# A long-convolution generator on one core: phases and exponents as pairs of PSUM banks, with exponential and absolute value in one operation of 1024 columns

## The chip, the core and the metric

The kernel runs on one core of a Trainium2 chip. A core has a matrix engine (TensorE, PE in the profile; its weight loads are PEld), a vector engine (VectorE, DVE), an engine for functions of one operand (ScalarE, ACT), a general one (GpSimd, POOL) and one that issues transfers (SyncE, SP). Each works through its own queue in order, and waits for others through semaphores. TensorE writes its results to PSUM, which has eight banks of 512 float32 columns in each of 128 partitions; the other operands lie in SBUF. The metric is the time of one execution on the device, in microseconds.

## The reference, cut to what matters

All is float32, for 2048 tokens of 448 channels. The first half is a state-space convolution, of which the kernel K is what the change touches:

```python
dt = jnp.exp(log_dt)
A = -jnp.exp(log_A_real) + 1j * A_imag              # 448 x 256
C = (C_real + 1j * C_imag) * dt[:, None]
P = jnp.exp((A * dt[:, None])[:, :, None] * pos)    # pos = 0 .. 2047
K = 2.0 * jnp.einsum("dn,dnl->dl", C, P).real       # 448 x 2048
y = irfft(rfft(u_t, 4096) * rfft(K, 4096))[:, :, :2048]
```

Around it stand a modulation (`silu(c) @ w_mod`, cut into six vectors), a layer norm ahead of the convolution, a gated residual, a second layer norm, and a two-layer perceptron over the tokens (2048 to 1792 to 2048, with gelu), gated into the residual.

## The kernel before, in words

**Generator.** A position is written as 64 j + i, so that P is a product of a part E (over j, 64 values) and a part G (over i, 32 values), each a magnitude times a cosine or sine. The 448 channels are 28 groups of 16, and a group's 256 states are two halves of 128 partitions; so there are 56 steps s, of 16 channels x 128 states each (16 channels x 32 values = 512 columns). A step needs two exponents (for E and G) and two phases (for E and G), each a full PSUM bank of 128 x 512.

- `st_exponents` (L612) has TensorE compute the exponents of E and of G from a small table and the parameters (`lex`), by `halves` (L606): partitions 0 to 63 of the operands give E's, 64 to 127 G's, two matmuls that can run side by side. `st_exp` (L617) has ScalarE take two exponentials, L621, into one SBUF tile `mag` of 2 x 512 columns.
- `st_phase` (L623) gives the phases in turns, reduced to within half a turn by adding and subtracting a large constant in PSUM: eight matmuls, four for each bank.
- `st_mag2` (L634) has GpSimd form `m2`, the magnitudes for the second half of E, in two operations (L637, L639).
- `st_step` (L642) has ScalarE take two absolute values (L651 of E's phase into `ab`, L652 of G's into a `gs` buffer) and four sines: E's sine (L653, in place in PSUM), G's sine (L654), G's cosine (L655) and E's cosine (L656, into G's phase bank), the cosines being sines of a quarter turn less the absolute value. GpSimd forms G by two products (L658, L659), VectorE E by four: L660 and L661 with the sine, then whatever `between()` has queued for VectorE, then L663 and L664 with the cosine.
- `st_kgen` (L676) multiplies G and E on TensorE into 32 x 64 blocks of K, which ScalarE copies out (L699); `st_s1` (L710) starts K's transform.

The PSUM pool `pph` has two buffers each of a bank `xe` and a bank `xg`, used in turn by exponents and phases; so phases of step s+2 reuse the banks of step s. `ab` has one buffer, `gs` three, `m2` three (and five more, `m2l`, from s = 32), `mag` eight.

**Order.** Exponentials and sines need different tables on ScalarE, so the steps are taken in seven windows of eight (`BATCH`): `window(s)` at s = 0, 8, ..., 48 takes eight exponentials, with TensorE one exponent ahead, and then eight steps follow. The order on TensorE, ScalarE, VectorE and GpSimd is that in which the program writes its instructions (a manual schedule); SP's order is left to the scheduler from s = 8 to the end of the generator. In iteration s the phases of s+1 are written ahead of step s; from s = 33 on, `st_kgen(s - 1)` is between them. Other work is written into the same queues: until s = 32 the parameters of the next channels (`chain`, in pieces on VectorE, with `split`, L379, whose two-part results `hl` are stored by SP's queue at L388 and come back as `lph` and `lex`), the modulation, the transform of the input (`u_rows`, `u_cols`), and from s = 32 the inverse transform of the first 224 channels (`piece`: `pc_s2` and `pc_inv` on TensorE, the products L786 on VectorE).

**After the generator**, from about 367 us of the span, come the inverse transform of the other channels, the second layer norm and the two large products of the perceptron (L1191 to L1193 and L1333 to L1335), each weight split into two parts by ScalarE (L206) and VectorE (L215).

Of the kernel before, what the change touches and what calls it, by code (L numbers as in the profile page):

```python
# [11 lines left out]
F32 = mybir.dt.float32  # L12
F32R = mybir.dt.float32r
# [9 lines left out]
P = 128  # L23
# [4 lines left out]
GD = 16  # L28
# [192 lines left out]
def tile_adaln_s4d_mixer(ctx, tc, i, out):  # L221
# [20 lines left out]
    with ExitStack() as es:  # L242
# [126 lines left out]
        def chain(q):  # L369
# [7 lines left out]
            )  # L377

            def split(src, places):  # L379
                hl = qp.tile([P, 2, N], F32R, tag="hl", name="hl", bufs=3)[:, :, 0:f]  # L380
                eng = G if aside else V
                eng.tensor_copy(hl[:, 0], src)
                yield
                eng.tensor_tensor(hl[:, 1], src, hl[:, 0].bitcast(F32), ALU.subtract)
                for k, v in places:
                    for m in range(P // n):
                        to = pars[q][v, k, 0:n, :, m * f : (m + 1) * f]
                        nc.sync.dma_start(to, hl[n * m : n * m + n].bitcast(F32))  # L388
                yield
# [216 lines left out]
        def halves(out, lhs, rhs, start, stop):  # L606

            for k in range(2):
                r = slice(64 * k, 64 * k + 64)
                T.matmul(out[k], lhs[r], rhs[r], start=start, stop=stop)  # L610

        def st_exponents(s):  # L612
            g, h = divmod(s, 2)
            phs[s] = [pph.tile([P, 512], F32, tag=nm, name=nm) for nm in ("xe", "xg")]
            halves(phs[s], lex[g % 4][:, h * P : (h + 1) * P], tab[:, 2], True, True)

        def st_exp(s):  # L617
            mags[s] = mp.tile([P, 2, 512], F32, tag="mag", name="mag")
            pm = phs.pop(s)
            for k in range(2):  # L620
                S.activation(mags[s][:, k], pm[k], AF.Exp)  # L621

        def st_phase(s):  # L623

            g, h = divmod(s, 2)
            lhs = lph[g % 3][:, h * P : (h + 1) * P]
            pm = [pph.tile([P, 512], F32, tag=nm, name=nm) for nm in ("xe", "xg")]
            halves(pm, lhs, tab[:, 1], True, False)
            halves(pm, mg[:, 0], ones, False, False)
            halves(pm, mg[:, 1], ones, False, False)  # L630
            halves(pm, lhs, tab[:, 0], False, True)
            phs[s] = pm

        def st_mag2(s):  # L634
            me = v32(mags[s][:, 0])
            w = wp.tile([P, GD], F32, tag="w", name="w")
            G.tensor_tensor(w[:, :, None], me[:, :, 31:32], me[:, :, 1:2], ALU.mult)  # L637
            m2 = m2p[s >= 32 and s % BATCH > 2].tile([P, GD, 32], F32, tag="m2", name="m2")
            G.tensor_tensor(m2, me, w[:, :, None].to_broadcast([P, GD, 32]), ALU.mult)  # L639
            m2s[s] = m2  # L640

        def st_step(s, between):  # L642
            me, mg_, m2 = v32(mags[s][:, 0]), v32(mags[s][:, 1]), m2s.pop(s)
            E = gp_.tile([P, 2, GD, NJ], F32, tag="E", name="E")
            Gt = gp_.tile([P, 2, GD, NI], F32, tag="G", name="G")


            xe, xg = phs.pop(s)
            ab, sg, cg_ = (wp.tile([P, 512], F32, tag=nm, name=nm, bufs=b) for nm, b in (("ab", 1), ("gs", 3), ("gs", 3)))

            S.activation(ab, xe, AF.Abs)  # L651
            S.activation(cg_, xg, AF.Abs)  # L652
            S.activation(xe, xe, AF.Sin, scale=TWO_PI)  # L653
            S.activation(sg, xg, AF.Sin, scale=-TWO_PI)  # L654
            S.activation(cg_, cg_, AF.Sin, scale=-TWO_PI, bias=math.pi / 2)  # L655
            S.activation(xg, ab, AF.Sin, scale=-TWO_PI, bias=math.pi / 2)  # L656
            se, ce = v32(xe), v32(xg)
            G.tensor_tensor(Gt[:, 1], mg_, v32(sg), ALU.mult)  # L658
            G.tensor_tensor(Gt[:, 0], mg_, v32(cg_), ALU.mult)  # L659
            V.tensor_tensor(E[:, 1, :, 32:64], m2, se, ALU.mult)  # L660
            V.scalar_tensor_tensor(E[:, 1, :, 31::-1], me[:, :, 31::-1], -1.0, se, ALU.mult, ALU.mult)  # L661
            between()
            V.tensor_tensor(E[:, 0, :, 31::-1], me[:, :, 31::-1], ce, ALU.mult)  # L663
            V.tensor_tensor(E[:, 0, :, 32:64], m2, ce, ALU.mult)  # L664
            eg[s] = (E, Gt)
            mags.pop(s)
# [297 lines left out]
        def window(s):  # L964
# [13 lines left out]
            for e in range(BATCH):  # L978
# [37 lines left out]
                    piece(pieces[0] < NP)  # L1016
                if s == 0 and e in (4, 5):
                    st_mag2(e - 4)
                elif s and (e < 2 or s >= 32):
                    st_mag2(s + e)  # L1020
                if s == 8 and e == 0:
                    u_norm(e + 2)
# [13 lines left out]
        for s in range(tail):  # L1036
            if s == 32:
                early.close()
                fp = es.enter_context(tc.tile_pool(name="fp", bufs=2))
                m2p.append(right("m2l", BATCH - 3))  # L1040
                yks[1] = fp.tile([P, 32, DC], F32, name="yk1", bufs=1)
                for n in range(3):
                    pc_load(n)
# [44 lines left out]
            free = s > 7 and not st_s1(s % BATCH == BATCH - 1)  # L1088
            if s + 2 < 32 and (s + 2) % BATCH > 1:
                st_mag2(s + 2)  # L1090

            if 3 < s < 8:
                modulation(s // 2 - 1, s % 2)
# [273 lines left out]
```

## Time and profile before

| | |
|---|---|
| time, median of 3 runs | 719.54 us (715.1 to 722.51) |
| the profiled execution, its own time | 720.75 us |
| its span, first to last instruction | 719.0 us |
| mean granted TensorE clock | 0.962 |
| busy: PE, ACT, DVE, POOL | 648.0, 453.1, 431.4, 271.7 us |
| first and last L651 (absolute value of step 0, step 55) | 30.03 and 361.14 us |

A group's row names line, engine, operation, output <- input, shape and count, then busy time and mean duration (ns), and after the second bar the idle time of the engine just before and what ended most of it. A row of a timeline is: start in us from the span's beginning, duration in us, engine, line, operation, output <- input; in brackets, idle time before it and what ended it. The chain names the work that ended last, step by step back from the end. Durations of neighbours on one engine can overlap, so the distance from start to start says what an operation costs in a row of them.

### The profile page before, as it was taken

To read this page: it belongs to the slowest core of one execution; us is meant where nothing else is said; L and a number is where in the kernel's file an instruction comes from. 1 tells how busy PE (TensorE), PEld (TensorE's weight loads), DVE (VectorE), ACT (ScalarE), POOL (GpSimd) and SP (SyncE) were. 2 spreads that over 40 slices of the span, in tenths; PEclk is the share of its full clock that TensorE was granted. 3 is DMA by queue.
4 is the path that set the end of the run, shared out by engine and by line. 5 is a ranking of instruction groups with operands and counts; after the bars stand their busy time and mean duration, and the time that the engine had idled before them with its cause. 6 is when DMAs were issued, how large, how long until landed. Compare 5 with 4: busy or idle time off the path is not lost.

```text
span 719.0 us, 18067 instructions
## 1 busy us (share of the span) xinstructions
PE 648.0 (90%) x7090; PEld 479.3 (67%) x7090; DVE 431.4 (60%) x821; ACT 453.1 (63%) x849; POOL 271.7 (38%) x341
## 2 busy tenths in 40 slices
PE   0777999879979879898999979999999999999997
PEld 0443444435535556575679936778999999999996
DVE  7668768758577567584855448778622263334441
ACT  4877487887986989999947649787522242222220
POOL 5395657548656866867745600000000000000000
PEclk9998758998999989999999999999999999999999
DMA  8494545556867656555459999984585436555540
GB/s 196 154 200 130 194 141 178 204 162 197 250 194 237 186 119 178 147 156 156 137 156 282 296 255 251 248 218 115 171 231 150 145 110 175 168 159 154 154 142 26
DMA packets 99395, 128.00 MB, mean 178 GB/s; under 512 B 13546, under 2 KB 80622, under 8 KB 99310
## 3 DMA queue, kind: packets, MB, share of 16 engines
q1 hardware_dynamic: 97726, 122.78, 60.3%
q0 software_dynamic: 1008, 3.54, 2.2%
q8 instruction: 56, 0.92, 0.6%
q10 hardware_dynamic: 576, 0.52, 0.3%
q14 instruction: 29, 0.24, 0.1%
HBM read 91.46 MB, written 34.87 MB: 176 GB/s over the span
## 4 chain that ended last, share of the span: by engine, by line
PE 65%; ACT 12%; DMA 9%; DVE 6%; issue 3%; POOL 3%; SPq 1%; DVEq 0%; ACTq 0%; POOLq 0%
PE acc L1191 6%; PE o L1333 6%; PE o L1335 6%; PE o L1334 6%; PE acc L1193 6%; PE acc L1192 6%; PE xe L610 6%; PE kg L685 4%; DMA wm<-in_w_mod_dram 4%; PE vv L794 3%; PE kx L778 3%; PE vv L795 3%; PE pu L563 2%; PE xg L610 2%; PE pm L487 2%
## 5 line engine op out<-in xcount | busy, mean ns | idle before, releaser
L206 ACT CAST whi<-w 128x896 fp32r<-128x896 f32 x64 | 59.8, 937 | 135.5 <-PE o L1334 84.8
L658 POOL TENSOR_TENSOR G<-mag,gs 128x512 f32<-128x512 f32 x56 | 72.0, 1286 | 69.3 <-ACT gs L654 69.1
L215 DVE TENSOR_TENSOR wlo<-w,whi 128x896 fp32r<-128x896 f32 x64 | 68.0, 1086 | 43.2 <-ACT whi L206 37.0
L1191 PE MATMUL acc<-h3h,whi 128*128 128x448 f32 x224 | 82.8, 370 | 0.8 <-ACT h3h L1242 0.8
L1192 PE MATMUL acc<-h3l,whi 128*128 128x448 f32 x224 | 80.9, 361 | 0.7 <-DVE h3l L1249 0.5
L1193 PE MATMUL acc<-h3h,wlo 128*128 128x448 f32 x224 | 81.3, 363 | 0.0
L1333 PE MATMUL o<-uh,whi 128*128 128x448 f32 x224 | 81.3, 363 | 0.0
L1335 PE MATMUL o<-uh,wlo 128*128 128x448 f32 x224 | 81.2, 362 | 0.0
L1334 PE MATMUL o<-ul,whi 128*128 128x448 f32 x224 | 80.6, 360 | 0.0
L610 PE MATMUL xg<-tab,lph 64*128 64x512 f32 x112 | 66.7, 597 | 12.6 <-DVE E L664 7.7
L685 PEld LDWEIGHTS kg<-E,G 128*32 128x32 f32 x3584 | 56.7, 115 | 31.1 <-issue 16.4
L610 PE MATMUL xe<-tab,lph 64*128 64x512 f32 x112 | 65.7, 592 | 9.3 <-ACT gs L655 7.6
L659 POOL TENSOR_TENSOR G<-mag,gs 128x512 f32<-128x512 f32 x56 | 71.8, 1282 | 0.0
L685 PE MATMUL kg<-E,G 128*32 128x64 f32 x3584 | 66.5, 229 | 3.4 <-ACT ks L699 2.0
L660 DVE TENSOR_TENSOR E<-m,xe 128x512 f32<-128x512 f32 x56 | 38.4, 686 | 46.6 <-ACT xe L653 30.3
L639 POOL TENSOR_TENSOR m<-mag,w 128x512 f32<-128x512 f32 x56 | 58.7, 1049 | 4.4
L1337 DVE SCALAR_TENSOR_TENSOR y<-o,b,mod 128x448 f32<-128x448 f32 x16 | 11.0, 685 | 80.2 <-PE o L1335 80.2
L1191 PEld LDWEIGHTS acc<-h3h,whi 128*128 128x128 f32 x224 | 42.0, 188 | 12.8 <-ACT h L1247 5.6
L786 DVE TENSOR_TENSOR z<-kx,u 128x448 f32<-128x448 f32 x48 | 28.4, 620 | 32.5 <-PE kx L778 32.5
L610 PE MATMUL xe<-tab,lex 64*128 64x512 f32 x56 | 29.8, 544 | 19.7 <-DMA lex<-wm 18.1
L651 ACT ACTIVATE ab<-xe 128x512 f32<-128x512 f32 x56 | 33.9, 606 | 17.4 <-PE xg L610 9.9
L1192 PEld LDWEIGHTS acc<-h3l,whi 128*128 128x128 f32 x224 | 41.9, 187 | 4.1 <-DVE h3l L1249 0.8
(221 smaller groups left out, 1514.7 us busy)
## 6 DMA issues: line engine op xcount, KB each, us to landing
w<-in_B_w_dram SPq DMA_DIRECT2D x64, 224.0 KB
w<-in_B_w_dram SPq DMA_DIRECT2D x32, 448.0 KB
u<-us_d SPq DMA_DIRECT2D x48, 224.0 KB
yu_d<-yt SPq DMA_DIRECT2D x16, 448.0 KB
yi<-yu_d SPq DMA_DIRECT2D x32, 224.0 KB
us_d<-uo SPq DMA_DIRECT2D x16, 448.0 KB
v_d<-vt SPq DMA_DIRECT2D x32, 224.0 KB
vt<-v_d SPq DMA_DIRECT2D x16, 448.0 KB
```

What stands on the lines that cost most here:

```text
L206: self.nc.scalar.copy(hi, w)
L215: eng.tensor_tensor(lo, w, hi.bitcast(F32), ALU.subtract)
L610: T.matmul(out[k], lhs[r], rhs[r], start=start, stop=stop)
L658: G.tensor_tensor(Gt[:, 1], mg_, v32(sg), ALU.mult)
L659: G.tensor_tensor(Gt[:, 0], mg_, v32(cg_), ALU.mult)
L685: T.matmul(kgs[g][32 * q : 32 * q + 32, m], Gt[:, c, d], E[:, c, d], start=h == 0 and c == 0 and m == 0, stop=h == 1 and c == 1, skip_grou ...
L1191: nc.tensor.matmul(acc[f], hi[:, fs], h3h[:, r], start=r == 0, stop=False)
L1192: nc.tensor.matmul(acc[f], hi[:, fs], h3l[:, r], start=False, stop=False)
L1193: nc.tensor.matmul(acc[f], lo[:, fs], h3h[:, r], start=False, stop=r == 15)
L1333: nc.tensor.matmul(o, hi[:, ks], uh[kh][:, k], start=kh == 0 and k == 0, stop=False)
L1334: nc.tensor.matmul(o, hi[:, ks], ul[kh][:, k], start=False, stop=False)
L1335: nc.tensor.matmul(o, lo[:, ks], uh[kh][:, k], start=False, stop=kh == 1 and k == 6)
```

## The change

E's and G's banks become one tile `x` of two banks, from one pool tag with two buffers (the same four banks). One exponential and one absolute value of 2 x 512 columns take the place of two each. The four sines stay as they were, but the two cosines read their absolute value from the one tile `ab`, which is twice as large, with one buffer. To make room in SBUF, `hl` has two buffers in place of three and `m2l` four in place of five; for that, `m2` of the last step of each window from s = 32 is formed after the window's third step and not inside `window`.

```diff
-                hl = qp.tile([P, 2, N], F32R, tag="hl", name="hl", bufs=3)[:, :, 0:f]
+                hl = qp.tile([P, 2, N], F32R, tag="hl", name="hl", bufs=2)[:, :, 0:f]
...
-                T.matmul(out[k], lhs[r], rhs[r], start=start, stop=stop)
+                T.matmul(out[:, k], lhs[r], rhs[r], start=start, stop=stop)
 
         def st_exponents(s):
             g, h = divmod(s, 2)
-            phs[s] = [pph.tile([P, 512], F32, tag=nm, name=nm) for nm in ("xe", "xg")]
+            phs[s] = pph.tile([P, 2, 512], F32, tag="x", name="x")
...
         def st_exp(s):
             mags[s] = mp.tile([P, 2, 512], F32, tag="mag", name="mag")
-            pm = phs.pop(s)
-            for k in range(2):
-                S.activation(mags[s][:, k], pm[k], AF.Exp)
+            S.activation(mags[s], phs.pop(s), AF.Exp)
 
         def st_phase(s):
...
-            pm = [pph.tile([P, 512], F32, tag=nm, name=nm) for nm in ("xe", "xg")]
+            pm = pph.tile([P, 2, 512], F32, tag="x", name="x")
...
-            m2 = m2p[s >= 32 and s % BATCH > 2].tile([P, GD, 32], F32, tag="m2", name="m2")
+            m2 = m2p[s >= 32 and 2 < s % BATCH < 7].tile([P, GD, 32], F32, tag="m2", name="m2")
...
-            xe, xg = phs.pop(s)
-            ab, sg, cg_ = (wp.tile([P, 512], F32, tag=nm, name=nm, bufs=b) for nm, b in (("ab", 1), ("gs", 3), ("gs", 3)))
-
-            S.activation(ab, xe, AF.Abs)
-            S.activation(cg_, xg, AF.Abs)
+            x = phs.pop(s)
+            xe, xg = x[:, 0], x[:, 1]
+            ab = wp.tile([P, 2, 512], F32, tag="ab", name="ab", bufs=1)
+            sg, cg_ = (wp.tile([P, 512], F32, tag="gs", name="gs", bufs=3) for _ in range(2))
+
+            S.activation(ab, x, AF.Abs)
             S.activation(xe, xe, AF.Sin, scale=TWO_PI)
             S.activation(sg, xg, AF.Sin, scale=-TWO_PI)
-            S.activation(cg_, cg_, AF.Sin, scale=-TWO_PI, bias=math.pi / 2)
-            S.activation(xg, ab, AF.Sin, scale=-TWO_PI, bias=math.pi / 2)
+            S.activation(cg_, ab[:, 1], AF.Sin, scale=-TWO_PI, bias=math.pi / 2)
+            S.activation(xg, ab[:, 0], AF.Sin, scale=-TWO_PI, bias=math.pi / 2)
...
-                elif s and (e < 2 or s >= 32):
+                elif s and (e < 2 or s >= 32 and e < 7):
                     st_mag2(s + e)
...
-                m2p.append(right("m2l", BATCH - 3))
+                m2p.append(right("m2l", BATCH - 4))
...
+            if 32 <= s < NHALF and s % BATCH == 2:
+                st_mag2(s + 5)
```

In the changed kernel the line numbers from there on differ by one or two: the exponential is L619, the operations of a step on ScalarE are L651 (absolute value), L652 to L655 (sines), VectorE's products L659, L660, L662, L663, and GpSimd's G products L657, L658.

## Prediction

> **What bounds the kernel now.** I read the page's chain first, then its groups of instructions for the lines that the diff touches, then the timelines of ScalarE, VectorE and TensorE over one window of the generator, because the change lies in the generator alone (up to about 367 us of the span) and a share of the whole span says nothing about it.
>
> ```profile
> PE 65%; ACT 12%; DMA 9%; DVE 6%; issue 3%; POOL 3%; SPq 1%; DVEq 0%; ACTq 0%; POOLq 0%
> L660 DVE TENSOR_TENSOR E<-m,xe 128x512 f32<-128x512 f32 x56 | 38.4, 686 | 46.6 <-ACT xe L653 30.3
> L651 ACT ACTIVATE ab<-xe 128x512 f32<-128x512 f32 x56 | 33.9, 606 | 17.4 <-PE xg L610 9.9
> L206 ACT CAST whi<-w 128x896 fp32r<-128x896 f32 x64 | 59.8, 937 | 135.5 <-PE o L1334 84.8
> ```
>
> TensorE carries most of the chain, but most of that is the two big products after the generator, which the change only moves in time. In the generator the second row matters: VectorE, before its first product of a step, waits mostly (30.3 us of 46.6) for the FIRST sine of that step, L653, the third of ScalarE's six operations. The next fences show the last window of eight steps (s = 48 to 55). T(s) is the start of a step's L651.
>
> ```profile
> 334.76 0.60 ACT L651 ACTIVATE ab<-xe 128x512 f32<-128x512 f32 x1
> ...
> 338.66 0.60 ACT L656 ACTIVATE xg<-ab 128x512 f32<-128x512 f32 x1
> 339.30 0.60 ACT L651 ACTIVATE ab<-xe 128x512 f32<-128x512 f32 x1
> ...
> 341.77 0.61 ACT L656 ACTIVATE xg<-ab 128x512 f32<-128x512 f32 x1
> 342.30 0.55 ACT L800 COPY vt<-vv 128x448 f32<-128x448 f32 x1
> 342.72 0.62 ACT L651 ACTIVATE ab<-xe 128x512 f32<-128x512 f32 x1
> 343.20 0.63 ACT L652 ACTIVATE gs<-xg 128x512 f32<-128x512 f32 x1
> ...
> 344.19 0.64 ACT L654 ACTIVATE gs<-xg 128x512 f32<-128x512 f32 x1
> ...
> 345.19 0.65 ACT L656 ACTIVATE xg<-ab 128x512 f32<-128x512 f32 x1
> ...
> 349.79 0.63 ACT L651 ACTIVATE ab<-xe 128x512 f32<-128x512 f32 x1
> ...
> 357.23 0.63 ACT L651 ACTIVATE ab<-xe 128x512 f32<-128x512 f32 x1
> 361.14 0.61 ACT L651 ACTIVATE ab<-xe 128x512 f32<-128x512 f32 x1
> ```
>
> Two things are to be seen. First, operations of ScalarE that need not wait overlap: L651 starts at 342.72, lasts 0.62, and L652 starts at 343.20, 0.48 later. Second, an operation that waits for the one just before it loses that overlap: L656 at 341.77 is followed after 0.53 by a copy that does not need it, but L656 at 338.66 is followed after 0.64 by L651, which must wait until the single buffer of `ab` has been read. A step's last sine ends at 345.84, T + 3.12.
>
> ```profile
> 339.90 0.68 DVE L664 TENSOR_TENSOR E<-m,xg 128x512 f32<-128x512 f32 x1
> 344.42 0.69 DVE L660 TENSOR_TENSOR E<-m,xe 128x512 f32<-128x512 f32 x1 [0.71 <-ACT xe L653]
> 347.28 0.68 DVE L664 TENSOR_TENSOR E<-m,xg 128x512 f32<-128x512 f32 x1
> 354.34 0.68 DVE L664 TENSOR_TENSOR E<-m,xg 128x512 f32<-128x512 f32 x1
> ```
>
> ```profile
> 340.69 0.47 PE L610 MATMUL xg<-tab,lph 64*128 64x512 f32 x1 [0.97 <-DVE E L664]
> 348.16 0.50 PE L610 MATMUL xe<-tab,lph 64*128 64x512 f32 x1
> 348.76 0.58 PE L610 MATMUL xg<-tab,lph 64*128 64x512 f32 x1
> ```
>
> This is the loop that sets the pace of the steps, beside ScalarE's own work: there are two sets of phase banks, so the phases of step s+2 need the banks that the products of step s read last (L664). From the end of L664 to TensorE's next matmul is 0.11 us (339.90 + 0.68 = 340.58 to 340.69), the eight matmuls of a step take 1.18 (348.16 to 349.34), and ScalarE starts about 0.05 later: 1.34 us from the end of L664 to T(s+2) at the least.
>
> **The change part by part.** *One operation of 1024 columns for two of 512.* From 512 to 896 columns an operation goes from 606 to 937 ns, 0.86 ns a column, so 1024 columns are estimated at 1.05 us. Less the overlap of 0.13 that is 0.92 against two starts of 0.48: 0.04 saved per pair, 56 exponentials and 56 absolute values, 4.5 us if ScalarE set the pace everywhere. For the exponentials the gain lies between 0 and 56 x 0.04 = 2.2; TensorE shares the exponential windows, so I take 1.0.
>
> On ScalarE, the Trainium skill ("ScalarE: Activation LUTs", section "What ACT_TABLE_LOAD costs") gives 186 ns + 0.833 ns a column and an overlap of about 93 ns, so that a pair would save 93 ns: about 10 us over 112 pairs. The trace agrees with the page's duration (606 against 612), but its overlap here is 0.14, so less is left to save.
>
> *What the pair waits for.* The two banks are now one tile, `x`. The built program's order of ScalarE and VectorE, with each one's waits, shows what that does:
>
> ```
> ACT  L651 ab<-x     waits PE, and ACT L655 of the step before
> ACT  L652 x<-x      waits DVE (two steps back), and ACT L651, the operation just before
> ACT  L653 gs<-x     waits POOL, and ACT L652, the operation just before
> ACT  L654 gs<-ab    waits POOL
> ACT  L655 x<-ab     waits ACT L653
> DVE  L659 E<-m,x    waits ACT L655, the last sine of the step
> DVE  L660 E<-mag,x  no wait
> DVE  L662 E<-mag,x  no wait
> ```
>
> In the kernel before, the first product waited for L653 and the third for L656. Now all four stand behind the last sine, and two more of ScalarE's operations wait for their neighbour. A step on ScalarE becomes: absolute value 1.05 + 0.03, first sine 0.64, second 0.48, third 0.52, last 0.62 to its end, so the last sine ends at T + 3.34 where it was T + 3.12: 0.22 longer. VectorE's first product starts at T + 3.38 where it was T + 1.70 (344.42 - 342.72): 1.68 late, and with it the end of the products, since the work between them (the z products of L786, of the chain, of the evacuations) is queued behind the first two and starts as late. Where the third product already waited for the last sine (steps with nothing between), the delay is ScalarE's 0.22 and two products of about 0.6 (0.69 less some overlap), 1.4; in the first step of a window, where the table load stands before the sines and the last one moves from T + 4.50 (338.66 + 0.60 - 334.76) to T + 4.60, 1.30, and up to 1.68 where work lies between. Behind the waiting product stand, on VectorE's queue, the evacuations that TensorE needs; behind the phase matmuls on TensorE's queue stand `kgen` and the inverse transforms.
>
> *What of 1.68 reaches the next step but one.* T(s+2) moves by the delay less the slack, and the slack is T(s+2) less the end of L664 less 1.34. Last window: s = 48, 342.72 - 340.58 - 1.34 = 0.80, so 1.30 - 0.80 = 0.50; s = 50, 349.79 - 347.96 - 1.34 = 0.49, so 1.19; s = 52, 357.23 - 355.02 - 1.34 = 0.87, so 0.81. Sum 2.5, and 0.22 for the odd step at the end: 2.7. The window of s = 40 has the same rhythm, 26.36 against 361.14 - 334.76 = 26.38, so 2.7 again; that of s = 32 is 28.06 long for other waits, which can hide up to 1.7 of it; I take 1.7, between 1.0 and 2.7.
>
> ```profile
> 250.66 0.60 ACT L651 ACTIVATE ab<-xe 128x512 f32<-128x512 f32 x1
> ...
> 278.72 0.60 ACT L651 ACTIVATE ab<-xe 128x512 f32<-128x512 f32 x1
> 293.55 0.61 ACT L651 ACTIVATE ab<-xe 128x512 f32<-128x512 f32 x1
> ...
> 319.91 0.61 ACT L651 ACTIVATE ab<-xe 128x512 f32<-128x512 f32 x1
> ```
>
> The four windows before s = 32 have other bounds between, so only the tight loops count:
>
> ```profile
> 101.76 0.67 DVE L664 TENSOR_TENSOR E<-m,xg 128x512 f32<-128x512 f32 x1
> ...
> 124.54 0.68 DVE L664 TENSOR_TENSOR E<-m,xg 128x512 f32<-128x512 f32 x1
> ...
> 160.27 0.68 DVE L664 TENSOR_TENSOR E<-m,xg 128x512 f32<-128x512 f32 x1
> ...
> 226.80 0.68 DVE L664 TENSOR_TENSOR E<-m,xg 128x512 f32<-128x512 f32 x1
> ...
> 235.71 0.67 DVE L664 TENSOR_TENSOR E<-m,xg 128x512 f32<-128x512 f32 x1
> ```
>
> ```profile
> 103.56 0.60 ACT L651 ACTIVATE ab<-xe 128x512 f32<-128x512 f32 x1 [0.15 <-PE xe L610]
> ...
> 127.19 0.60 ACT L651 ACTIVATE ab<-xe 128x512 f32<-128x512 f32 x1
> ...
> 162.79 0.60 ACT L651 ACTIVATE ab<-xe 128x512 f32<-128x512 f32 x1 [1.31 <-PE xe L610]
> ...
> 230.35 0.60 ACT L651 ACTIVATE ab<-xe 128x512 f32<-128x512 f32 x1 [0.61 <-PE xe L610]
> ...
> 237.49 0.60 ACT L651 ACTIVATE ab<-xe 128x512 f32<-128x512 f32 x1 [0.75 <-PE xe L610]
> ```
>
> Window 24: from s = 27 the slack is 230.35 - 227.48 - 1.34 = 1.53, 0.15 comes through; from s = 29 it is 237.49 - 236.38 - 1.34 = -0.23 (TensorE there began one bank before the other was free, which a pair cannot), so 1.9; with 0.22, 2.3. Window 16: 162.79 - 160.95 - 1.34 = 0.50 after a first step, 1.1. Window 8: from s = 8, 103.56 - 102.43 - 1.34 = -0.21, 1.8, of which the queue on VectorE passes on about half by s = 13; there 127.19 - 125.22 - 1.34 = 0.63 lets 1.05 more through: 2.1. Window 0 ends in a wait for the modulation weights,
>
> ```profile
> 40.88 19.11 DMA wm<-in_w_mod_dram
> ```
>
> whose transfer starts once an early step has freed a table row on SP's queue: between 0 and 1.7, I take 0.4. After the last step the products end 1.4 later than 364.88 + 0.68 = 365.56, at 367.0, and `kgen`, which began at 365.89 behind GpSimd, begins about 1.2 later.
>
> ```profile
> 364.88 0.68 DVE L664 TENSOR_TENSOR E<-m,xg 128x512 f32<-128x512 f32 x1
> ...
> 365.89 0.93 PEld L685 LDWEIGHTS kg<-E,G 128*32 128x32 f32 x62 [0.41 <-POOL G L659]
> ```
>
> *The rest of the diff* pays for the larger `ab` with memory and I cost it at nothing. `hl` with two buffers makes a split wait for the store of two splits back instead of three; the chain's own arithmetic on VectorE lies between them and covers it; without that cover it is one store's landing on GpSimd per split. The late `st_mag2` of e = 7 goes to GpSimd's queue behind a step's G products, where GpSimd waits for the next sines anyway; without cover, one product per window. SP's order changes by a few places around s = 8 to 20, past loads that are needed a window later. Let each be worth 1 us either way.
>
> *Sum:* 0.4 + 2.1 + 1.1 + 2.3 + 1.7 + 2.7 + 2.7 + 1.2 - 1.0 = 13.2 us later at the end of the generator, and what follows is moved as a whole. The profiled execution took 720.75 (a span of 719.0 and 1.75 around it), 1.2 above the median of three, 719.54; so 734.0 by the one and 732.7 by the other. I say 733.5.
>
> **The rivals.** *Fewer instructions win (faster).* If the two banks were guarded apart, VectorE would start after the first sine as before, and only the saving would be left: 112 x 0.04 = 4.5, about 715. It decides if VectorE's first product starts under T + 2. Against it stands the order above, where the third product has no wait of its own. By the skill's overlap this rival would stand near 710. The Trainium skill ("PSUM — Partial Sum Buffer", "PSUM bank collisions raise a hardware error") asks for guards by bank and quadrant only, under which this rival would hold; the order shows guards wider than that. 0.05.
>
> *The delay is hidden (no change).* TensorE's own queue may be what each step waits for, and give the slack back: then only ScalarE's 0.22 in the 24 steps from s = 32 (5.3) and part of the end remain, at most 6, 722 to 726. For it: outside the tight loops the slacks are large, as 1.53 above. 0.17.
>
> *It spreads (slower still).* TensorE's queue is in order; if what stands behind the phases (inverse transforms, evacuations) gives no slack back, 1.7 comes through in three loops of each of seven windows: 36 us, 756; half of it, 18, and ScalarE's 5.3 give 744. 0.12.
>
> **How the numbers follow.** The forecast, 727 to 742, has 0.66. One per cent, about what a measurement of this kernel can tell from no change, is 712.3 to 726.7. Slower holds the forecast and the spreading: 0.78; the hidden delay is "same", 0.17; faster 0.05. The range takes in the upper part of the hidden case and the half-spread one: 725 to 746.
>
> **What would show it.** VectorE's group of the first product should name the last sine as its releaser and wait some 40 us or more for it, not 30.3. The 1024-column absolute value should last about 1.05 us, and each of the next two sines start after its predecessor's end. The windows of s = 40 and 48 should be 29 us long from first to last step, not 26.4. If they are 26.4 or less, the loop was not the bound and the forecast is wrong; if ScalarE sits idle before the 1024-column operations for TensorE by more than 1.5 us a step, the spreading is right.

## The result and the profile after

The changed kernel takes 752.0 us (median of 6 runs, 748.88 to 757.72); the kernel before takes 719.46 beside it (6 runs, 715.1 to 722.51). The ratio is 1.0458, with a 95% interval of 1.0417 to 1.05: it is slower, as forecast, but by 32.5 us and not by 13 to 14, and 752.0 lies over the range of 725 to 746. The profiled execution is the slowest of the six: 757.72 us, a span of 755.9, and a mean granted clock of 0.930 where it was 0.962 before. Where sizes matter I therefore go by stretches of the generator, and compare them over several kernels.

The first fence is from the page of the kernel after: the chain of work that ended last, and the groups that the change touches.

```profile
PE 60%; ACT 15%; DMA 9%; DVE 7%; issue 5%; POOL 3%; SPq 0%; ACTq 0%; DVEq 0%; POOLq 0%
L659 DVE TENSOR_TENSOR E<-m,x 128x512 f32<-128x512 f32 x56 | 38.5, 687 | 95.3 <-ACT x L655 49.1
L651 ACT ACTIVATE ab<-x 128x1024 f32<-128x1024 f32 x56 | 57.5, 1028 | 32.9 <-PE x L610 32.6
L619 ACT ACTIVATE mag<-x 128x1024 f32<-128x1024 f32 x56 | 55.6, 1026 | 23.8 <-PE x L610 20.0
```

VectorE's wait before its first product has doubled, 46.6 to 95.3 us. The page puts 49.1 of it down to L655, the step's last sine, and no longer to the first; the timeline shows the rest to be the same wait: the first product never starts before the last sine has ended, and in 53 of the 56 steps it starts 0.03 to 0.20 us after it, where in the kernel before it starts ahead of that end in 53 steps. The operations of 1024 columns last 1.03 us. The idle time before the absolute value, nearly all of it for TensorE, has grown from 17.4 to 32.9. The next three fences are timelines of the kernel after in the window of s = 40: ScalarE, VectorE and TensorE from the start of step 44 (T = 332.41) to that of step 45.

```profile
332.41 1.03 ACT L651 ACTIVATE ab<-x 128x1024 f32<-128x1024 f32 x1
333.48 0.58 ACT L652 ACTIVATE x<-x 128x512 f32<-128x512 f32 x1
334.15 0.60 ACT L653 ACTIVATE gs<-x 128x512 f32<-128x512 f32 x1
334.64 0.62 ACT L654 ACTIVATE gs<-ab 128x512 f32<-128x512 f32 x1
335.17 0.59 ACT L655 ACTIVATE x<-ab 128x512 f32<-128x512 f32 x1
337.06 0.37 ACT L698 COPY ks<-kg 128x256 f32<-128x256 f32 x1 [1.30 <-PE kg L684]
337.33 1.03 ACT L651 ACTIVATE ab<-x 128x1024 f32<-128x1024 f32 x1
```

```profile
333.95 0.68 DVE L663 TENSOR_TENSOR E<-m,x 128x512 f32<-128x512 f32 x1
335.85 0.69 DVE L659 TENSOR_TENSOR E<-m,x 128x512 f32<-128x512 f32 x1 [1.21 <-issue]
```

```profile
334.78 0.50 PE L610 MATMUL x<-tab,lph 64*128 64x512 f32 x2 [1.18 <-ACT gs L653]
335.09 0.60 PE L610 MATMUL x<-ones,mg 64*128 64x512 bf16 x3
...
335.89 1.10 PE L684 MATMUL kg<-E,G 128*32 128x64 f32 x64
```

Within a step all is as worked out: the absolute value 1.03, the first sine 0.04 after its end, the second 0.09 after the end of the first, the last sine done at 335.76 (T + 3.35, forecast T + 3.34), the first product at 335.85 (T + 3.44, forecast T + 3.38). What is new is the row before the last of ScalarE. It has nothing to do with the sines: L698 copies out a block of K, and stands in ScalarE's queue ahead of the next absolute value. Step 43's products end at 334.63, TensorE starts the phases of step 45 at 334.78, and these are there from about 336; but behind them on TensorE stands `kgen` of step 43, to 336.99, and ScalarE waits 1.30 us for it with the copy at the head of its queue. In the tables of ScalarE's waits (us in total, times, longest) this wait has nearly doubled; the first line is of the kernel before, the second of the kernel after:

```profile
ACT ks L699 <- PE kg L685: 9.3, 11, 2.5
ACT ks L698 <- PE kg L684: 17.7, 13, 2.4
```

From the end of the products to the next step but one are 337.33 - 334.63 = 2.70 us, not 1.34.

### The profile page after: what moved, and what is told of

It reads as the page before. It is cut to its first block, busy times and chain, and to the rows that moved or that the text cites. A ratio compares the mean times of both kernels' runs of the same rounds, so it can differ in the third digit from the quotient of the medians.

```text
span 755.9 us, 17908 instructions
## 1 busy us (share of the span) xinstructions
PE 653.7 (86%) x7090; PEld 480.1 (64%) x7090; DVE 426.7 (56%) x821; ACT 457.8 (61%) x737; POOL 272.5 (36%) x341
## 4 chain that ended last, share of the span: by engine, by line
PE 60%; ACT 15%; DMA 9%; DVE 7%; issue 5%; POOL 3%; SPq 0%; ACTq 0%; DVEq 0%; POOLq 0%
PE x L610 8%; PE acc L1192 6%; PE o L1334 6%; PE o L1336 6%; PE o L1335 6%; PE acc L1194 6%; PE acc L1193 6%; PE kg L684 5%; ACT ab L651 5%; DMA wm<-in_w_mod_dram 3%; PE pu L531 2%; ACT gs L653 2%; ACT x L652 2%; PE pm L487 2%; PE kx L777 2%
## 5 line engine op out<-in xcount | busy, mean ns | idle before, releaser
L610 PE MATMUL x<-tab,lph 64*128 64x512 f32 x224 | 73.5, 647 | 43.9 <-ACT gs L653 18.2
L657 POOL TENSOR_TENSOR G<-mag,gs 128x512 f32<-128x512 f32 x56 | 71.7, 1280 | 99.1 <-ACT gs L653 98.7
L659 DVE TENSOR_TENSOR E<-m,x 128x512 f32<-128x512 f32 x56 | 38.5, 687 | 95.3 <-ACT x L655 49.1
L684 PEld LDWEIGHTS kg<-E,G 128*32 128x32 f32 x3584 | 61.3, 123 | 31.9 <-issue 23.3
L651 ACT ACTIVATE ab<-x 128x1024 f32<-128x1024 f32 x56 | 57.5, 1028 | 32.9 <-PE x L610 32.6
L684 PE MATMUL kg<-E,G 128*32 128x64 f32 x3584 | 71.0, 239 | 1.6 <-DVE E L663 1.1
L658 POOL TENSOR_TENSOR G<-mag,gs 128x512 f32<-128x512 f32 x56 | 71.8, 1282 | 0.0
L610 PEld LDWEIGHTS x<-tab,lph 64*128 64x128 f32 x224 | 27.1, 227 | 70.0 <-ACT gs L653 24.1
L619 ACT ACTIVATE mag<-x 128x1024 f32<-128x1024 f32 x56 | 55.6, 1026 | 23.8 <-PE x L610 20.0
L610 PE MATMUL x<-tab,lex 64*128 64x512 f32 x112 | 32.3, 567 | 29.7 <-DMA lex<-wm 18.8
L785 DVE TENSOR_TENSOR z<-kx,u 128x448 f32<-128x448 f32 x48 | 28.4, 620 | 31.2 <-PE kx L777 31.2
```

What stands on the lines that cost most here:

```text
L610: T.matmul(out[:, k], lhs[r], rhs[r], start=start, stop=stop)
L651: S.activation(ab, x, AF.Abs)
L684: T.matmul(kgs[g][32 * q : 32 * q + 32, m], Gt[:, c, d], E[:, c, d], start=h == 0 and c == 0 and m == 0, stop=h == 1 and c == 1, skip_grou ...
```

## The experiments

Twelve more kernels ran. The table gives for each the ratio to the kernel before on the same chip, and, from its trace, the time from the first to the last L651 of some of the windows, and in the last column the gap from the last L651 of the window of s = 24 to the first of the next.

| kernel | us, ratio (95%) | s=8 | s=16 | s=24 | s=32 | s=40 | s=48 | gap |
|---|---|---|---|---|---|---|---|---|
| before | 719.46 | 32.4 | 30.1 | 34.4 | 28.1 | 26.4 | 26.4 | 13.2 |
| after | 752.0, 1.0458 (1.0417 to 1.05) | 39.1 | 31.1 | 37.0 | 32.1 | 31.9 | 32.6 | 18.0 |
| 1 before, cosine first | 744.07, 1.0352 (1.0272 to 1.0432) | 37.5 | 30.7 | 34.7 | 31.2 | 32.0 | 32.4 | 15.4 |
| 2 after, singles | 754.2, 1.0475 (1.0418 to 1.0531) | 37.6 | 31.8 | 34.9 | 33.3 | 32.9 | 32.7 | 19.0 |
| 3 before, memory | 720.62, 1.0004 (0.9977 to 1.0031) | 32.4 | 30.0 | 35.0 | 27.6 | 26.4 | 27.6 | 13.2 |
| 4 after, copy later | 744.68, 1.0335 (1.0285 to 1.0386) | 35.9 | 31.3 | 37.2 | 30.1 | 29.7 | 29.0 | 18.3 |
| 5 after, sine apart | 763.54, 1.0586 (1.0535 to 1.0638) | 40.1 | 35.7 | 38.8 | 31.0 | 32.0 | 31.0 | 18.4 |
| 5c after, room alone | 760.49, 1.0553 (1.0514 to 1.0593) | 39.2 | 31.4 | 36.1 | 32.1 | 31.9 | 32.6 | 19.1 |
| 6 after, both apart | 800.61, 1.1118 (1.1051 to 1.1185) | 44.6 | 41.1 | 41.0 | 35.0 | 36.3 | 36.3 | 14.3 |
| 7 before, both apart | 798.97, 1.1119 (1.1051 to 1.1186) | 42.2 | 41.2 | 41.1 | 35.0 | 35.2 | 36.1 | 14.4 |
| 8 after, other work first | 746.26, 1.0372 (1.0314 to 1.0431) | 31.4 | 29.7 | 36.2 | 33.6 | 32.4 | 32.6 | 18.0 |
| 9 after, 8 and 4 | 736.72, 1.0211 (1.0146 to 1.0277) | 31.4 | 30.1 | 36.4 | 29.3 | 29.3 | 29.2 | 18.0 |
| 10 before, copy later | 719.75, 0.9991 (0.9962 to 1.002) | 30.5 | 30.5 | 34.4 | 26.1 | 26.0 | 25.5 | 14.6 |
| 11 after, products early, 4 | 761.46, 1.0595 (1.0557 to 1.0633) | 37.0 | 34.9 | 36.7 | 32.8 | 33.2 | 33.2 | 18.0 |

The theory on trial (A): the two banks under one guard put all four products behind the last sine; that and what it pushes back in three in-order queues is the loss. The rivals: the long operation itself; the memory edits; the pair of banks, which can only be refilled as a whole.

**1. The products late, without any pair.** In the kernel before, VectorE takes the two products with the cosine first:

```diff
-            V.tensor_tensor(E[:, 1, :, 32:64], m2, se, ALU.mult)
-            V.scalar_tensor_tensor(E[:, 1, :, 31::-1], me[:, :, 31::-1], -1.0, se, ALU.mult, ALU.mult)
-            between()
             V.tensor_tensor(E[:, 0, :, 31::-1], me[:, :, 31::-1], ce, ALU.mult)
             V.tensor_tensor(E[:, 0, :, 32:64], m2, ce, ALU.mult)
+            between()
+            V.tensor_tensor(E[:, 1, :, 32:64], m2, se, ALU.mult)
+            V.scalar_tensor_tensor(E[:, 1, :, 31::-1], me[:, :, 31::-1], -1.0, se, ALU.mult, ALU.mult)
```

> The kernel before with nothing paired; VectorE's four products of a step stand in the other order, the two with the cosine first, so that all four stand behind the step's last sine. Theory A (the late products set the new time: in the changed kernel the first product starts at T + 3.4 and not T + 1.7): the first product starts at about T + 3.15 here, 1.45 late where the change makes it 1.68, so 1.45/1.68 of the 32.5 us comes back: 740 to 750. Rival B (ScalarE's longer step, its waits for its own neighbour and the 1024-column operations set it): 719 to 726. Rival C (the memory edits and SP's order): 719 to 722.

It took 744.07. Its page has the wait:

```profile
L660 DVE TENSOR_TENSOR E<-mag,xg 128x512 f32<-128x512 f32 x56 | 38.5, 687 | 87.1 <-ACT xg L656 87.0
```

No bank is paired here and no operation lengthened, and yet 3.5 of the 4.6% are there; the windows of s = 40 and 48 are as long as those of the kernel after. Late products alone do most of it. The other 8 us (752.0 against 744.07) lie, by the two profiles, mainly in the windows and gaps up to s = 32; that they come from the pair being refilled only as a whole is likely, but no run here shows it.

**2. The pair without the long operations:** the two exponentials and the two absolute values single again, in the tile of two banks.

```diff
-            S.activation(ab, x, AF.Abs)
+            S.activation(ab[:, 0], xe, AF.Abs)
+            S.activation(ab[:, 1], xg, AF.Abs)
```

> The changed kernel with its two-bank tiles, but exponentials and absolute values as two operations of 512 columns each again. Theory A: the tile, not the long operation, holds the products back, so the time stays at 748 to 756. Rival B (the long operation itself, which lets neither bank go before both are done): back towards the kernel before, 720 to 735.

754.2, and its interval holds the 1.0458 of the kernel after. The long operations are neither the loss nor a gain that can be measured.

**3. The memory edits alone,** in the kernel before (`hl` 2, `m2l` 4, the last `m2` of a window later).

```diff
-                hl = qp.tile([P, 2, N], F32R, tag="hl", name="hl", bufs=3)[:, :, 0:f]
+                hl = qp.tile([P, 2, N], F32R, tag="hl", name="hl", bufs=2)[:, :, 0:f]
...
-                m2p.append(right("m2l", BATCH - 3))
+                m2p.append(right("m2l", BATCH - 4))
```

> The kernel before with the memory edits alone: two hl buffers, four m2l buffers, the last m2 of a window later. Theories A and B: 716 to 723. Rival C (these edits cost a part of the 32.5 us): 724 or more.

1.0004: nothing, as costed.

**4. The copy of K out of the way.** In the kernel after, from s = 33, L698's copy is queued behind the next step's absolute value.

```diff
-                act.append(copy)
+                act.append((lambda: hold.append(copy)) if s > 32 else copy)
...
             S.activation(ab, x, AF.Abs)
+            flush(hold)
```

> The changed kernel, but from s = 33 on ScalarE's copy of K's blocks (L698) is written behind the next step's absolute value and not ahead of it. In the changed kernel's trace that copy waits 1.3 to 2.4 us for TensorE ten times, with the next step behind it. Theory A2 (this copy on ScalarE's queue is the second half of the loss in the last three windows): 742 to 747. If the steps are set by the products alone: 750 to 753.

744.68, and the ratio falls from 1.0458 to 1.0335. ScalarE's timeline, steps 44 and 45 of this run:

```profile
327.17 1.03 ACT L651 ACTIVATE ab<-x 128x1024 f32<-128x1024 f32 x1
...
329.92 0.59 ACT L656 ACTIVATE x<-ab 128x512 f32<-128x512 f32 x1
330.80 1.03 ACT L651 ACTIVATE ab<-x 128x1024 f32<-128x1024 f32 x1 [0.29 <-PE x L610]
331.79 0.37 ACT L699 COPY ks<-kg 128x256 f32<-128x256 f32 x1
```

The copy no longer waits, and the next step begins 3.63 us after the one before, not 4.92. The windows from s = 32 lose 1.9 to 3.6 us each; those of s = 8, 16 and 24, where the copy is not moved, are still 3.5, 1.2 and 2.8 us over the kernel before.

**5, 5c, 6, 7. The sines out of the pair, into SBUF.** I wanted to undo the guard and keep the pair: E's sine into a tile `es` of its own (5), E's cosine too, into `ec` (6), the same with single banks (7), and only the edits that make room for `es` (5c). This is 5; 6 does the same with the cosine:

```diff
-            S.activation(xe, xe, AF.Sin, scale=TWO_PI)
+            es_ = wp.tile([P, 512], F32, tag="es", name="es", bufs=1)
+            S.activation(es_, xe, AF.Sin, scale=TWO_PI)
...
-            se, ce = v32(xe), v32(xg)
+            se, ce = v32(es_), v32(xg)
...
-                yts[R, gp] = xp.tile([P, 2, D], F32, tag="yt", name="yt", bufs=3)
+                yts[R, gp] = xp.tile([P, 2, D], F32, tag="yt", name="yt", bufs=2)
```

> The kernel after, but E's sine goes to an SBUF tile of its own in place of E's phase bank; to make room, two buffers instead of three for yt and three instead of four for m2l. The pair of banks, the operations of 1024 columns and the place of the cosine stay. Theory (the one guard of the two-bank tile puts the first product behind the last sine and makes two sines wait for their neighbour): the first product starts near T + 1.7 to 2.3 again, and 716 to 728 comes out. Rival (the pair of banks itself is what costs, since no phase bank can be refilled before the whole pair is read): 745 or more, since the cosine still lies in the pair and holds it until the last product.

> The kernel after with only the edits that make room for the experiment with E's sine apart (yt 2 buffers, m2l 3 with two magnitudes formed later). If the room costs nothing, 749 to 756, as the kernel after; if it costs, the difference is to be taken off the others of this call.

> The kernel after, with E's sine and E's cosine both in SBUF tiles of their own (room: yt 2, st 1, m2l 2 buffers). The pair of phase banks is then released by ScalarE's last sine and not by VectorE's last product. Theory (the loop runs from the products over the phase banks to the next step but one): the loop is cut, ScalarE's own 3.6 us a step sets the pace, the windows of s = 40 and 48 become 25 to 27 us long from first to last step, and 700 to 716 comes out, under the kernel before. Rival (the kernel before was bound by the copies of K on ScalarE's queue behind TensorE, not by the phase banks): 717 to 726, no better than the kernel before.

> The kernel before (single banks, single operations of 512 columns) with E's sine and cosine in SBUF tiles of their own. It tells what the pairing itself is worth once nothing is held by VectorE. Theory: within 6 us of the kernel with pairs and both apart, and slower than it by up to 112 x 0.04 = 4.5 us. If it comes out faster than that by more than 3 us, pairs of banks cost even without the guard on the products; if it stays at 717 to 722, the gain of the other needs the pairs.

The theories of 5 (716 to 728) and 6 (700 to 716) failed; 5 fell to its rival's "745 or more", and 5c to the case that the room costs. Of 7, that it lies within 6 us of 6 came true, both far above what I thought. The room costs some 7 us itself (1.0553 against 1.0458): with two buffers of `yt`, VectorE's waits in 5c have a row for their store that the kernel after has not.

```profile
DVE yt L534 <- DMA yu_d<-yt: 6.3, 6, 3.0
```

Beyond that, moving the sines gave nothing (5: 763.54, against 760.49 with the room alone) or cost some 40 us more (6: 800.61); 7 lies 79 us over the kernel before. The first product did start earlier, at T + 1.60 to 1.63 in 13 steps of 5, but look at how long the products take. From the page of 5:

```profile
L661 DVE SCALAR_TENSOR_TENSOR E<-mag,es 128x512 f32<-128x512 f32 x56 | 92.9, 1658 | 0.0
L660 DVE TENSOR_TENSOR E<-m,es 128x512 f32<-128x512 f32 x56 | 55.8, 996 | 28.8 <-ACT es L653 27.0
```

and from the timelines of VectorE and GpSimd in 6, both sines in SBUF:

```profile
357.88 1.76 DVE L661 TENSOR_TENSOR E<-m,es 128x512 f32<-128x512 f32 x1
359.57 0.68 DVE L662 SCALAR_TENSOR_TENSOR E<-mag,es 128x512 f32<-128x512 f32 x1
360.17 0.68 DVE L664 TENSOR_TENSOR E<-mag,ec 128x512 f32<-128x512 f32 x1
360.77 0.68 DVE L665 TENSOR_TENSOR E<-m,ec 128x512 f32<-128x512 f32 x1
```

```profile
357.38 1.72 POOL L660 TENSOR_TENSOR G<-mag,gs 128x512 f32<-128x512 f32 x1
361.44 1.74 POOL L659 TENSOR_TENSOR G<-mag,gs 128x512 f32<-128x512 f32 x1 [2.35 <-ACT gs L654]
```

A product whose operands both lie in SBUF takes 0.68 us while GpSimd is idle (359.10 to 361.44) and up to 1.80 beside one of GpSimd's products; one with an operand in PSUM takes 0.68 in both cases, in the kernel before and after (L659 of the kernel after: 687 ns on average, and 55 of its 56 lie wholly beside work of GpSimd). The Trainium skill ("SBUF — State Buffer", section "Who interferes with whom") says that a VectorE instruction with two SBUF inputs contends with a GpSimd instruction that reads SBUF, and one with at most one SBUF input, outside the two-port modes, does not; the trace agrees, with 0.68 against 1.76. So these two operands are better off in PSUM, for a reason that no wait in the profile of before shows. It is not the only cost of 6 and 7: `es` and `ec` have one buffer each, and ScalarE waits 51.2 us (6) and 55.4 us (7) for VectorE's last product before it can write `ec` again. How much of the loss is the single buffer and how much the slow products was not separated, and these four runs say nothing for or against the guard. In 6 and 7, with and without pairs, the time is the same (1.1118 and 1.1119; the room differs by one buffer of `m2l`): pairing is worth nothing there either.

**8 and 9. VectorE's other work into its wait.** In the kernel after, `between()` goes ahead of the first product (8); the same with the copy later (9).

```diff
+            between()
             V.tensor_tensor(E[:, 1, :, 32:64], m2, se, ALU.mult)
             V.scalar_tensor_tensor(E[:, 1, :, 31::-1], me[:, :, 31::-1], -1.0, se, ALU.mult, ALU.mult)
-            between()
```

> The kernel after, with VectorE's other work (what between queues: the channels' chain, evacuations, z products) written ahead of the step's first product, and not between the second and the third. It runs while VectorE would wait for the last sine. Theory (the loss in the windows of s = 8 and 24 and in the gaps before s = 24 and 32 is VectorE's other work, late behind the waiting first product): 736 to 746, with the windows of s = 8 and 24 and the gap before s = 32 back within 2 us of the kernel before, and the steps with a z product about 1 us shorter from first product to last. Rival (TensorE's queue alone passes the delay on): the early windows stay, 748 to 754.

> The kernel after with both: the other work ahead of the first product, and from s = 33 the copies of K behind the next step's absolute value. If the two losses are separate, the gains add: 7 us under the run with the other work first alone, 728 to 740. If both are the same wait seen from two sides: no more than the better of the two.

8 took 746.26, just over the 736 to 746 of its theory, and 9 took 736.72, within its 728 to 740. In the window of s = 8 TensorE needs VectorE's evacuations L534 to go on; in the kernel after, they come behind two products that wait themselves:

```profile
122.83 0.69 DVE L659 TENSOR_TENSOR E<-m,x 128x512 f32<-128x512 f32 x1 [1.01 <-issue]
123.44 0.68 DVE L660 SCALAR_TENSOR_TENSOR E<-mag,x 128x512 f32<-128x512 f32 x1
124.03 1.68 DVE L534 TENSOR_TENSOR yt<-pu,mod 128x448 f32<-128x448 f32 x3
```

```profile
118.39 0.97 PE L531 MATMUL pu<-xt,wu 32*64 32x448 f32 x4
120.25 2.20 PE L531 MATMUL pu<-xt,wu 32*64 32x448 f32 x8 [0.89 <-DVE yt L534]
122.37 1.93 PE L684 MATMUL kg<-E,G 128*32 128x64 f32 x64
124.24 0.79 PE L610 MATMUL x<-tab,lph 64*128 64x512 f32 x2
```

TensorE waits 0.89 for an evacuation, and `kgen` and the next phases stand behind. But this is the only such wait in that window, so it is not the bulk of the loss there. VectorE's own time is the better account: before, it is busy for 27.2 of the window's 32.4 us, and in the kernel after its waits ahead of the first product grow in this window from 6.2 to 13.1 us, by about as much as the window does; in 8 they are 2.0. With the other work first, that window falls from 39.1 to 31.4, under the 32.4 of the kernel before. (Some of the 39.1 may belong to this one execution, whose granted clock there was 0.60, where it was 0.72 to 0.79 in 2, 4 and 5c; these have 37.6, 35.9 and 39.2 without the edit, and 8 has 31.4 at 0.78.) The windows from s = 32 gain nothing from 8 alone (33.6, 32.4 and 32.6): there the copy stands at the head of ScalarE's queue. With both edits 17.8 us are gone (1.0458 less 1.0211, of 719.46), at least the 8.9 and 6.2 that the ratios of 4 and 8 give: the gains add. In 9 the windows of s = 40 and 48 are 29.3 and 29.2 us long. In the later steps of such a window the rows show the loop of the prediction at its shortest, VectorE first and then ScalarE:

```profile
321.65 0.68 DVE L664 TENSOR_TENSOR E<-m,x 128x512 f32<-128x512 f32 x1
```

```profile
320.11 1.03 ACT L651 ACTIVATE ab<-x 128x1024 f32<-128x1024 f32 x1
323.75 1.03 ACT L651 ACTIVATE ab<-x 128x1024 f32<-128x1024 f32 x1 [0.30 <-PE x L610]
```

Step 43's products end at 321.65 + 0.68 = 322.33, and step 45 starts at 323.75, 1.42 later, where 1.34 was the least by the prediction: 0.30 of it is ScalarE's wait for the phases. Of the 2.9 us that this window still has over the kernel before, 2.6 arise earlier, in its first three steps (4.58 + 4.85 + 4.78 from start to start against 4.53 + 3.43 + 3.64). TensorE's rows show where, first in the kernel before, then in 9:

```profile
298.03 0.47 PE L610 MATMUL xe<-tab,lph 64*128 64x512 f32 x1 [1.43 <-ACT gs L655]
299.47 0.46 PE L610 MATMUL xg<-tab,lph 64*128 64x512 f32 x1 [0.97 <-DVE E L664]
300.55 1.10 PE L685 MATMUL kg<-E,G 128*32 128x64 f32 x64
```

```profile
309.25 0.80 PE L610 MATMUL x<-tab,lph 64*128 64x512 f32 x2 [4.25 <-ACT gs L654]
311.28 1.93 PE L685 MATMUL kg<-E,G 128*32 128x64 f32 x64
313.15 1.85 PE L778 MATMUL kx<-yk,si 128*128 128x224 f32 x4
```

With the products of the first step late, TensorE stands still for 4.25 us in one piece, and then works slowly: the eight phase matmuls take 2.11 us and not 1.18, `kgen` 1.93 and not 1.10, L778 1.85 and not the 1.02 of the next step. The granted clock of this stretch (309.2 to 315.0) is 0.51; in the kernel before it is 1.00 (298.0 to 303.2). The three differences add up to 2.6 us. The windows of s = 40 and 48 have the same in the kernel after and in runs 1, 2, 4, 8, 9 and 11: a pause of 4.04 to 4.40 us in the second step, then a `kgen` of 1.72 to 1.94 us. That the pause brings the low clock is not tested; the two stand together in all of these.

By its expectation, 8 should also have brought back the gap ahead of s = 32; that stays at 18.0, and this part of the theory is wrong. The window of s = 24, at 36.2, is within the 2 us.

**10. The same copy later in the kernel before.**

```diff
-                act.append(copy)
+                act.append((lambda: hold.append(copy)) if s > 32 else copy)
...
             S.activation(ab, xe, AF.Abs)
+            flush(hold)
```

> The kernel before, with the copies of K from s = 33 behind the next step's absolute value, as they were moved in the kernel after. In the kernel before ScalarE waits 9.3 us for TensorE ahead of the copies. If the copy holds up the next absolute value there too: 712 to 718. If it is hidden there (the wait fell on the path only once the products came late): 718 to 722.

719.75, 0.9991 (0.9962 to 1.002). Its table of ScalarE's waits has

```profile
ACT ks L700 <- PE kg L686: 1.7, 4, 0.6
```

(us in total, times, longest), where the kernel before had 9.3: the wait went and the time stayed. (In this profile the windows from s = 32 are 3.2 us shorter together, and the gaps ahead of them 2.7 longer.) So the copy's place is no flaw of the kernel before; it costs only once the products are late.

**11. The guard from the other side.** The kernel after with the copy later, and the first two products written ahead of the last sine in the program. Nothing but the order of writing is changed:

```diff
+            V.tensor_tensor(E[:, 1, :, 32:64], m2, se, ALU.mult)
+            V.scalar_tensor_tensor(E[:, 1, :, 31::-1], me[:, :, 31::-1], -1.0, se, ALU.mult, ALU.mult)
             S.activation(xg, ab[:, 0], AF.Sin, scale=-TWO_PI, bias=math.pi / 2)
```

> The kernel after with the copies of K later (as in the run of 744.68), and the first two products written ahead of the last sine in the program, so that they need only wait for G's sine; the sines stay in the pair of banks, in PSUM. Nothing but the order of writing is changed, so it shows what the one guard of a two-bank tile does in the other direction. Theory: the first product starts near T + 2.3 to 2.4 and not T + 3.43, but the last sine, which writes the same tile, now waits for the second product and ends near T + 4.2 in place of T + 3.3; a step is then at least 4.3 on ScalarE, and the windows of s = 40 and 48 are 30 to 31 us long: 740 to 748, no gain on 744.68. Rival (only VectorE's late start costs): 724 to 736, with windows of 27 to 28.

The mechanism came as expected, and the time was worse, 761.46 (1.0595), over the 740 to 748 expected. VectorE and ScalarE at step 46 (T = 348.59):

```profile
350.95 0.69 DVE L657 TENSOR_TENSOR E<-m,x 128x512 f32<-128x512 f32 x1 [1.40 <-ACT gs L654]
351.55 0.68 DVE L658 SCALAR_TENSOR_TENSOR E<-mag,x 128x512 f32<-128x512 f32 x1
```

```profile
350.81 0.63 ACT L655 ACTIVATE gs<-ab 128x512 f32<-128x512 f32 x1
352.33 0.60 ACT L659 ACTIVATE x<-ab 128x512 f32<-128x512 f32 x1 [0.89 <-DVE E L658]
352.96 1.02 ACT L651 ACTIVATE ab<-x 128x1024 f32<-128x1024 f32 x1
```

The first product starts at T + 2.36. The last sine writes the other bank of the tile, yet waits 0.89 us until the second product has read the first bank (351.55 + 0.68 = 352.23). ScalarE's waits have it in 54 of 56 steps:

```profile
ACT x L659 <- DVE E L658: 50.3, 54, 1.0
```
Each step then takes 4.4 to 4.8 us on ScalarE: it is now ScalarE that sets the pace. I had left out the copies in the steps of 4.84, and the first step of a window, 5.7. One guard over two banks makes one of the two engines wait, whichever is written first.

## Why the prediction was right in sign and wrong in size

- *The pair's guard.* Right. All products of a step wait for the last sine: by the timeline (the first product never starts before the end of L655, where it followed L653, the first sine) and by run 1, where lateness alone costs some 24 us.
- *A step on ScalarE.* Right within 0.06 us: the last sine's end and the first product's start are given with the first timelines. 1024 columns take 1.03 where 1.05 was estimated.
- *The memory edits at nothing.* Right (run 3).
- *The exponentials' gain of 1.0.* Wrong, and nothing was gained: ScalarE waits for TensorE in those gaps, and the gaps ahead of s = 40 and 48 went from 14.83 and 14.85 to 14.98 each. (In the pair of banks with single operations, run 2, they are 15.35 and 15.34: there the long operation does give 0.4 a gap.)
- *The slack, "T(s+2) less the end of L664 less 1.34".* This is the step that failed. It takes for granted that once the phases are there ScalarE can start. The text said that `kgen` stands behind the phases on TensorE's queue, but not who waits for it at the head of ScalarE's: the copy of K. The slack that I subtracted was filled by 1.10 us of `kgen` and 0.3 of the copy, so the distance was 2.70. The windows of s = 32, 40 and 48, put at 1.7 + 2.7 + 2.7 = 7.1, cost 4.0 + 5.5 + 6.2 = 15.7. With the copy moved (run 4) they cost 2.1 + 3.3 + 2.6 = 8.0, and with both moves (run 9) 1.3 + 2.9 + 2.8 = 7.0. What the copy did shows best from the fourth step of these windows on: there they cost 3.2 + 2.7 + 2.7 in the kernel after and 0.6 + 0.3 + 0.3 in run 9.
- *TensorE's eight phase matmuls at 1.18 everywhere.* Wrong, and no term of the sum stands for it: in the first steps of these windows they take up to 2.11, at a granted clock of 0.51 (run 9) to 0.70 (the window of s = 40 of the kernel after). By the durations of the phases, `kgen` and the four matmuls behind it that is 1.5 us in the window of s = 40 of the kernel after, 2.2 in that of s = 48, and 2.6 in run 9.
- *Windows of 29.* Those of s = 40 and 48 are 29.3 and 29.2 in run 9, but that they agree with the prediction is luck. By the sum 0.5 of the 2.7 comes in the first three steps and 2.2 after them; in run 9 it is 2.6 and 2.5 in the first three, mostly by the low clock, and 0.3 after.
- *"The evacuations that TensorE needs" behind the waiting product.* Named, and then priced only through the end of the products, at 2.1 for the window of s = 8. That window cost 6.7 in the profiled execution, and 3.5 to 6.8 in runs 2, 4 and 5c. Run 8 writes VectorE's other work ahead of the product, and the window falls under that of before; but TensorE waits only 0.9 us for an evacuation there, so it is VectorE's own waiting, not TensorE's, that the rows show. This comes near to the mechanism of the rival "it spreads", in one window of seven; another part of the excess came by the copy, which no rival had. The time, 752.0, lies between that rival's 744 and 756, yet its own sign did not come: ScalarE waits 32.6 + 20.0 us for TensorE ahead of the operations of 1024 columns, 0.94 a step and not 1.5.
- *The sum as a whole.* From the first to the last L651 the profile of the kernel after is 32.3 us longer than that of before: 26.1 in the windows, put at 13.0, and 6.2 in the gaps between them, put at -1.0. Three windows came near: s = 0, 16 and 24, put at 0.4, 1.1 and 2.3, cost 0.1, 1.1 and 2.6.
- *What is left.* With both moves the kernel takes 736.72, 3 us over the 733.5 of the sum. That is luck too: in run 9 the windows of s = 0 to 24, put at 5.9, cost nothing together, and the gaps cost 8.3. Of the loss that stays, the gap ahead of s = 32 (4.8 us more than before in runs 8, 9 and 11, 2.2 in run 1) is the largest single piece and was not in the sum. It seems to hang on the banks being held by the products: in run 6, with the pair, but with banks that ScalarE alone releases, the gap is 14.3. The rows show where it goes: in run 9 ScalarE waits in this gap 2.5 us for exponents and 1.5 for GpSimd's `m2`, at a granted clock of 0.72, and in the kernel after 1.1 and 3.0, at 0.88; before, it waits 0.2 in all, at 1.00. The products of step 31 end 1.5 us later after its start than in the kernel before (5.91 against 4.41); how the pair makes 4.8 of that, where single banks make 2.2, stays open.

No version beat the kernel before: run 10 equals it, and the best one with a pair (9) is 2.1% slower (1.5 to 2.8).

## What to carry to other kernels

When one tile takes the place of two, ask first what each engine's queue waits for, then what stands BEHIND the delayed instruction in every in-order queue, to the second hop: here product, phases, `kgen`, copy, next step. A slack may be subtracted only after naming everything that is queued inside it; the copy's wait of 9.3 us was in the profile of before, harmless there (run 10), and became about 9 us of path when the products came late (run 4). Look at the granted clock behind a pause that grows: here matmuls behind TensorE's pauses of over 4 us took up to 1.8 times as long, though that the pause was the reason is not shown. A wait that can't be removed is still room for work: moving what was queued behind the waiting product to the front of it got 6 us back.

## What the runs showed of the hardware that I had not expected

- A VectorE product with both operands in SBUF lasts 0.68 us alone and up to 1.80 beside GpSimd's products, whose own mean rises from 1280 to 1548 ns (L657 of after, L659 of run 6). With one operand in PSUM VectorE keeps its 0.68. Moving both sines from PSUM to SBUF, with one buffer each, cost more than the guard.

```profile
L659 POOL TENSOR_TENSOR G<-mag,gs 128x512 f32<-128x512 f32 x56 | 86.7, 1548 | 74.0 <-ACT gs L654 71.4
```

- Four exponentials of 1024 columns without a wait in the kernel after take 3.77 us together, so one follows the other after (3.77 - 1.02) / 3 = 0.92; pairs of 512 columns started every 0.48. The saving is 0.04 a pair, as estimated from the overlap, and it never reached the path.

```profile
258.81 3.77 ACT L619 ACTIVATE mag<-x 128x1024 f32<-128x1024 f32 x4
```
